# Smaller, spread loads of keys, values and queries, and later loads of the first expert's weights, in a kernel of attention and experts

## The chip, the cores and the metric

One core of a Trainium2 chip runs the kernel, with its five engines: TensorE (PE), VectorE (DVE), ScalarE (ACT), GpSimd (POOL) and SyncE (SP). SP computes nothing here and issues nearly all transfers. The metric is the device time of one execution in microseconds (us); the time of a kernel is the median of its runs.

## The reference, cut to what matters

```python
def attn(q, k, v):                       # (8, 8, 576, 64) each
    k_p = k.reshape(B, H, Sp, 8, D).mean(axis=3)      # keys pooled by 8
    v_p = v.reshape(B, H, Sp, 8, D).mean(axis=3)
    s = q @ k_p.T / sqrt(D)
    a = exp(s - max(s))
    return (a / sum(a)) @ v_p
x = attn(q, k, v)                        # 4608 tokens of 512
do = x @ w_skip > 0                      # only these tokens are computed
e = argmax(x[do] @ w_gate); gate = softmax(x[do] @ w_gate)[e]
y = gate * (relu(x[do] @ w1[e]) @ w2[e]) # 8 experts, 512 -> 1024 -> 512
out = x;  out[do] = x[do] + y
```

## The kernel before, in words

The 4608 tokens are 36 tiles of 128. The first part of the kernel (`attention`) runs a hand-made software pipeline with one turn per tile, t = 0 to 35. In turn t, TensorE makes the scores of tile t (L285), multiplies the exponentials of tile t - 2 with the pooled values (L325, L327) and transposes those of tile t - 1 (L309, L310). ScalarE copies the transposed exponentials out of PSUM (pT, L314) and takes the exponentials of tile t (e, L298); VectorE takes the minima before them (mn, L293) and normalises tile t - 3 (L341 to L346), whose 128x512 result SP stores to the output (L347). All engines run their instructions in the order in which the program was written, SP too: a transfer that waits holds up every transfer written behind it.

A batch b is 576 tokens, 4.5 tiles, and its first tile is FIRST[b] = 0, 4, 9, 13, 18, 22, 27, 31 (t0 below). For a batch there are loaded: the keys (L187, one transfer of 128 x 2304 floats, 1152 KB, into half of the tile `stage`), summed over 8 by four instructions of VectorE (kp, L194) in turns t0 - 5 to t0 - 2; the values (L206, 128 x 2048, 1024 KB, into the room of `hhi` or `hlo`, and two small ones, L208), summed by GpSimd (L216, L232) from turn t0 - 5 on. Queries come two tiles at a time (L270, 512 KB, into `qt`, `xhi` or `xlo`). A dictionary `loads` says in which turn a load is issued (`at(turn, f)`): keys at t0 - 8, values at t0 - 7, the queries of tiles 2i and 2i + 1 at 2i - 6, ahead of that turn's store.

The second part (`experts`) multiplies groups of tokens with an expert's weights. Those are split into a high and a low part, so each weight chunk (512 KB, eight chunks for an expert) is loaded to a slot of `stage` (L601 for the first expert), then copied by ScalarE (`high`, L607, two pieces of 128x512) and subtracted by GpSimd (`low`, L610, two pieces). The first expert's chunks come during the attention, in turns `wload(cc)` = 15, 17, 19, 21, 24, 26, 28, 30. Chunks 3, 4 and 5 use the slots of chunks 0, 1 and 2, so their loads wait until GpSimd has made the lows of those. The three planners `act`, `dve` and `gps` place such side work in turns by a ready turn, a last turn and a cost.

GpSimd also writes one row of a table for every token of a tile (L411, 33 such writes) as the routing of a group of tiles is done on VectorE; a small load of that table (L517, nids) waits for the first 18 tiles' writes, and GpSimd's L520 waits for it. After the attention GpSimd gathers from the table (L1064). From the ninth transfer on, each of SP's transfers waits on one of eight landing semaphores that are used in turn, so that at most eight transfers are under way.

Of the kernel before, what the change touches and what calls it, by code (L numbers as in the profile page):

```python
# [36 lines left out]
B, H, S, HD, POOL = 8, 8, 576, 64, 8  # L37
# [3 lines left out]
NT = NTOK // 128  # L41
# [7 lines left out]
LONG = max(SUMMED)  # L49
PICK, EARLY = 9, 18  # L50
PICKED = 15
LAST = 6
SCALE = 1.0 / (POOL * HD ** 0.5)
GMAX = max(GROUPS)
# [31 lines left out]
KL = SP - KM  # L86
# [17 lines left out]
def flat(ap):  # L104
    return ap.rearrange("p k n -> p (k n)")
# [51 lines left out]
def attention(tc, nc, q, k, vm, vr, cf, wg, w1, w2, whi, wlo, out, c, pay, offs, table, near, bufs, late, early, mb, fin, cfs):  # L157
    with ExitStack() as ctx:
# [19 lines left out]
        vls = [sp.tile([128, POOL, HD], F32, name=f"vl{i}") for i in range(2)]  # L178
        el = [sp.tile([128, 128], F32, name=f"el{i}") for i in range(2)]
        halves = [slice(hh * 64, hh * 64 + 64) for hh in range(2)]  # L180
        kts, kps, vts, vss, vTs, qts = {}, {}, {}, {}, {}, {}

        def load_k(b, gs=None):
            n = 4 * SP * POOL
            kts[b] = flat(stage)[:, b % 2 * n:b % 2 * n + n].rearrange("p (g k i) -> p g k i", g=4, i=POOL)
            if gs is None:
                nc.sync.dma_start(kts[b], k[b])  # L187
            for g in gs or ():
                nc.sync.dma_start(kts[b][:, g], k[b, :, g])

        def sum_k(b, g):
            if b not in kps:
                kps[b] = kp.tile([128, 4, SP], F32, name="kp")
            nc.vector.tensor_reduce(kps[b][:, g], kts[b][:, g], axis=AX.X, op=ALU.add)  # L194

        def keys(b, hh, gs=slice(0, 4)):

            r = halves[hh]
            nc.scalar.activation(kbd[b % 2][r, gs, hh * SP:(hh + 1) * SP], kps[b][r, gs], AF.Copy, scale=-SCALE)

        def load_v(b):
            vt = early("hhi" if b % 2 else "hlo", 128, POOL, 4 * HD)
            if b == 1:
                early("room1", 128, 8)
            vl = vls[b % 2]
            nc.sync.dma_start(vt, vm[b])  # L206
            for hh in range(2):
                nc.sync.dma_start(vl[hh * 64:hh * 64 + 4 * KL], vr[b, hh])  # L208
            vts[b] = vt, vl

        def sums(b):

            vt, vl = vts.pop(b)
            vss[b] = vs = vp.tile([128, 4 * HD], F32, name="vs")
            ls = wide[:, b % 2]
            add = lambda y, x, z: lambda: nc.gpsimd.tensor_tensor(y, x, z, ALU.add)  # L216
            first = [add(vt[:, i:i + 2], vt[:, i:i + 2], vt[:, i + 4:i + 6]) for i in (0, 2)]
            if b == 0:
                def half():
                    nc.vector.tensor_reduce(vs[:, 0:128], vt[:, :, 0:128].rearrange("p i n -> p n i"), axis=AX.X, op=ALU.add)  # L220

                def other(o):
                    for i in range(POOL):
                        nc.tensor.matmul(o, ident, vt[:, i, 128:256], start=(i == 0), stop=(i == POOL - 1))
                    nc.scalar.activation(vs[:, 128:256], o, AF.Copy)

                first = half, other
            else:
                first += [add(vt[:, 0:2], vt[:, 0:2], vt[:, 2:4]), add(vs, vt[:, 0], vt[:, 1])]
            small = [add(vl[:, 0:4], vl[:, 0:4], vl[:, 4:8]), add(vl[:, 0:2], vl[:, 0:2], vl[:, 2:4]),  # L230
                     add(ls, vl[:, 0], vl[:, 1]),
                     lambda: nc.gpsimd.tensor_tensor(vl4[b % 3][:, :, 0:HD], ls.unsqueeze(1).broadcast_to([128, 4, HD]),  # L232
                                                     left.unsqueeze(2).broadcast_to([128, 4, HD]), ALU.mult)]
            return first, small
# [12 lines left out]
        def values_in(b, gs=slice(0, 4), by=None):  # L247
            (by or nc.gpsimd.tensor_copy)(vb[b % 2][:, gs, 0:HD], vss[b].rearrange("p (g d) -> p g d", d=HD)[:, gs])
# [16 lines left out]
        def load_q(i, part=0):  # L265
            s = 128, QG, 4, 128
            if i not in qts:
                qts[i] = qp.tile(list(s), F32, name="qt") if i % 4 < 2 else early("xlo" if i % 4 > 2 else "xhi", *s)
            sl = (slice(None), slice(0, 1), slice(1, QG))[part]
            nc.sync.dma_start(qts[i][:, sl], q[i, :, sl])  # L270
# [46 lines left out]
        def values(t, pT, apart=False):  # L317
            if apart:
                os = [ps_s.tile([128, 512], F32, name="sc") for _ in range(2)]
            else:  # L320
                o = ps_o.tile([128, 2, 512], F32, name="o")
                os = [o[:, 0], o[:, 1]]
            for g in range(4):
                for hh, r, sl, b in blocks(t):
                    nc.tensor.matmul(os[hh][sl, g * VA:(g + 1) * VA], pT[r, g, sl], vb[b % 2][r, g, :], start=(g == 0), stop=False)  # L325
            for hh, r, sl, b in blocks(t):
                nc.tensor.matmul(os[hh][sl, 0:4 * VA], pT[r, 4, sl], vl4[b % 3][r].rearrange("p g c -> p (g c)"), start=False, stop=True)  # L327
            return [o_.unsqueeze(1) for o_ in os] if apart else [o]
# [268 lines left out]
        def room(cc):  # L597
            return 5 + cc % 3 if cc < 6 else cc - 6

        def load_first(cc):  # L600
            nc.sync.dma_start(chunk_view(stage[:, room(cc)], cc), chunk_src(w1, w2, expert(0), cc))  # L601

        def piece(w, cc, i):
            return w[0][:, cc, i * 512:i * 512 + 512] if cc < 4 else w[1][:, (cc - 4) * 2 + i, :]

        def high(cc, i):
            nc.scalar.activation(piece(whi, cc, i), stage[:, room(cc), i * 512:i * 512 + 512], AF.Copy)  # L607

        def low(cc, i, by=nc.gpsimd):
            return by.tensor_tensor(piece(wlo, cc, i), stage[:, room(cc), i * 512:i * 512 + 512],  # L610
                                    piece(whi, cc, i).bitcast(F32), ALU.subtract)
# [82 lines left out]
        act, dve, gps = Work(ACT), Work(DVE), Paced(GPS)  # L694

        def at(t, f):
            loads.setdefault(t, []).append(f)
# [3 lines left out]
        def later_low(cc, i):  # L701
            if cc * 2 + i > 12:
                rest.append(lambda v: low(cc, i, v))
            else:
                gps.add((now["t"] + 1, NT - 6, NT - 6, NT - 1, NT - 1)[max(cc - 2, 0)], wload(cc + 3) - 1 if cc < 3 else (NT - 3, NT - 1, NT + 9, NT + 9)[cc - 3],
                        1.25, lambda: low(cc, i))

        def adds(b, ready, last):
            first, small = sums(b)
            if b == 0:  # L710
                return first, small
            fs = [first[0], first[1], small[0], first[2], small[1], first[3], small[2], small[3]]
            for f, cost in zip(fs, (1.25, 1.25, 0.7, 1.25, 0.45, 0.7, 0.3, 0.7)):
                gps.add(ready, last, cost, f)

        def wload(cc):
            return PICKED + 9 * cc // 4 if cc < 8 else NT - 2

        for b in range(1, B):
            t0, slow = FIRST[b], int(b == 1)  # L720
            if b > 1:
                at(t0 - 8, lambda b=b: load_k(b))
                at(t0 - 7, lambda b=b: load_v(b))
            for g in range(4):
                dve.add([2, 2, 3, 3][g] if slow else t0 - 5 + g + (b == 2 and g < 2), [2, 2, 3, 3][g] if slow else t0 - 5 + g + (b == 2 and g < 2), 0.7,
                        lambda b=b, g=g: sum_k(b, g))
            for hh in range(2):
                act.add(t0 - 1 + slow / 2, t0 - 1, 0.45, lambda b=b, hh=hh: keys(b, hh))
            at(t0 - 6 + 5 * slow, lambda b=b, t0=t0, slow=slow: adds(b, t0 - 5 + 4 * slow, t0 - 3 + 3 * slow))
            turns[t0 + slow] = b  # L730
            gps.add(t0 - 2 + 3 * slow, t0 - 1 + 2 * slow, 0.6, lambda b=b: values_in(b))
        for i in range(2, NT // QG):
            at(max(2 * i - 6, i // 2 - 1), lambda i=i: load_q(i))
        at(PICKED, lambda: nc.sync.dma_start(cfs[:, 128:320], cf[:, -192:]))
        for cc in range(8):
            at(wload(cc), lambda cc=cc: load_first(cc))
            for i in range(2 if cc < LAST else 0):
                act.add(wload(cc) + (3 if cc < 3 else 4), min(wload(cc) + 6, NT - 2), 0.55, lambda cc=cc, i=i: (high(cc, i), later_low(cc, i)))

        nc.gpsimd.memset(init, NO_TOKEN)  # L740
        load_k(0, [0])
# [186 lines left out]
        os_[NT - 1] = values(NT - 1, pts.pop(NT - 1), True)  # L928
        for cc in range(LAST, 8):
            for i in range(2):  # L930
# [790 lines left out]
```

## Time and profile before

| what | value |
|---|---|
| time, median of 3 runs | 486.68 us (485.38 to 490.21) |
| time of the profiled execution | 490.18 us |
| its span, first to last instruction | 488.4 us |
| TensorE busy | 461.8 us (95%) |
| VectorE, ScalarE, GpSimd busy | 286.2, 234.3, 203.2 us |
| SP's transfers | 25728 packets, 71.73 MB, 40.8% of 16 DMA engines' span |

The span lies 1.8 us inside the time of the same execution. The attention fills the first 140 us or so, and the experts the rest. Every other time below is read from this one execution.

### The profile page before, as it was taken

The numbers are of one execution on the slowest core, as the hardware profiler recorded it, in microseconds if no ns is written. First come the engines' busy times: TensorE is split into PE (matmuls) and PEld (weight loads), VectorE is DVE, ScalarE is ACT, GpSimd is POOL, SyncE is SP. The second block draws the span as 40 slices with busy tenths as digits, with TensorE's granted clock in tenths as the row PEclk, the third lists the DMA queues.
The fourth block names the chain that finished last, engine by engine and source line by source line (L and its number), as shares of the span: only waits on it lengthen the run. The fifth ranks groups of instructions, "written<-read, shape, count | busy, mean of one in ns | idle before, by whom it ended". The sixth has DMA issues, their size and how long they took to land. (4 is left out here: it accounts for less than half of the span.)

```text
span 488.4 us, 12498 instructions
## 1 busy us (share of the span) xinstructions
PE 461.8 (95%) x4232; PEld 400.2 (82%) x4233; DVE 286.2 (59%) x690; ACT 234.3 (48%) x614; POOL 203.2 (42%) x267
## 2 busy tenths in 40 slices
PE   8999899998998898999999999999999999999993
PEld 7777677766678687898989989899998989889872
DVE  3678988888768445267666746323236452635563
ACT  4788798998772024154544624112215321424350
POOL 4588469988884331242303024331323322033020
PEclk9999999999999998999999999999999999999998
DMA  8999899967420174657571646111114551234110
GB/s 290 399 399 398 314 374 403 381 219 240 142 68 25 51 269 130 234 162 255 171 274 65 224 167 217 50 43 43 40 44 138 204 173 58 90 137 138 70 42 10
DMA packets 33214, 87.29 MB, mean 179 GB/s; under 512 B 6751, under 2 KB 7263, under 8 KB 31249
## 3 DMA queue, kind: packets, MB, share of 16 engines
q1 hardware_dynamic: 25728, 71.73, 40.8%
q0 software_dynamic: 7440, 14.99, 9.4%
q8 instruction: 24, 0.39, 0.3%
q14 instruction: 22, 0.17, 0.1%
HBM read 72.58 MB, written 20.19 MB: 190 GB/s over the span
## 5 line engine op out<-in xcount | busy, mean ns | idle before, releaser
L1376 PE MATMUL psl<-xhi,w1hi 128*128 128x256 f32 (+3 forms) x352 | 103.5, 294 | 0.3 <-PEq L1155 0.3
L1377 PE MATMUL psl<-xlo,w1hi 128*128 128x256 f32 (+3 forms) x352 | 103.4, 294 | 0.0
L1378 PE MATMUL psl<-xhi,w1lo 128*128 128x256 f32 (+3 forms) x352 | 103.4, 294 | 0.0
L1282 POOL DMA_INDIRECT out<-ring,slot x34 | 35.3, 1039 | 162.0 <-POOLq L1155 146.9
L1502 ACT ACTIVATE hhi<-psl 128x256 fp32r<-128x256 f32 (+3 forms) x88 | 36.2, 411 | 110.6 <-ACTq L1155 105.7
L1575 DVE SCALAR_TENSOR_TENSOR hlo<-psl,hhi 128x256 fp32r<-128x256 f32 (+1 forms) x88 | 38.1, 434 | 59.1 <-DVEq L1155 56.1
L298 ACT ACTIVATE e<-sc,mn 128x72 f32<-128x72 f32 x288 | 64.9, 343 | 12.0 <-DVE mn L293 11.7
L1376 PEld LDWEIGHTS psl<-xhi,w1hi 128*128 128x128 f32 x352 | 66.1, 188 | 1.1 <-issue 0.7
L1377 PEld LDWEIGHTS psl<-xlo,w1hi 128*128 128x128 f32 x352 | 66.1, 188 | 0.4
L1378 PEld LDWEIGHTS psl<-xhi,w1lo 128*128 128x128 f32 x352 | 66.1, 188 | 0.0
L1492 ACT ACTIVATE xhi<-psd 128x512 fp32r<-128x512 f32 x36 | 19.1, 599 | 77.5 <-ACTq L1155 77.5
L1277 POOL DMA_INDIRECT ring<-out,slot x36 | 40.3, 1119 | 21.2 <-issue 16.5
L1398 PE MATMUL psf<-w2hi,hhi 128*128 128x512 f32 x96 | 38.8, 404 | 2.3 <-PEq L1155 2.3
L1552 DVE TENSOR_TENSOR w2lo<-stage,w2hi 128x1024 fp32r<-128x1024 f32 x28 | 34.2, 1225 | 9.4 <-DVEq L1155 8.9
L411 POOL DMA_INDIRECT table<-pay,r_di x33 | 32.9, 996 | 15.0 <-DVE p_two L436 8.1
L1399 PE MATMUL psf<-w2lo,hhi 128*128 128x512 f32 x96 | 38.2, 398 | 0.0
L1400 PE MATMUL psf<-w2hi,hlo 128*128 128x512 f32 x96 | 37.9, 395 | 0.0
L293 DVE TENSOR_REDUCE mn<-sc 128x4 f32<-128x288 f32 x72 | 30.5, 452 | 10.4 <-PE sc L285 5.7
L1552 DVE TENSOR_TENSOR w1lo<-stage,w1hi 128x1024 fp32r<-128x1024 f32 x28 | 32.4, 1220 | 3.4 <-DVEq L1155 3.3
L1399 PE MATMUL mb<-w2lo,hhi 128*128 128x512 f32 x88 | 34.3, 390 | 0.0
L1398 PE MATMUL mb<-w2hi,hhi 128*128 128x512 f32 x88 | 34.3, 390 | 0.0
L1400 PE MATMUL mb<-w2hi,hlo 128*128 128x512 f32 x88 | 34.3, 390 | 0.0
(299 smaller groups left out, 943.3 us busy)
## 6 DMA issues: line engine op xcount, KB each, us to landing
stage<-in_w SPq DMA_DIRECT2D x64, 512.0 KB
out<-x SPq DMA_DIRECT2D x36, 256.0 KB
stage<-in_k SPq DMA_DIRECT2D x7, 1152.0 KB
qt<-in_q SPq DMA_DIRECT2D x9, 512.0 KB
hlo<-in_vm SPq DMA_DIRECT2D x4, 1024.0 KB
hhi<-in_vm SPq DMA_DIRECT2D x4, 1024.0 KB
xhi<-in_q SPq DMA_DIRECT2D x4, 512.0 KB
xlo<-in_q SPq DMA_DIRECT2D x4, 512.0 KB
```

Of the source, the lines that this page charges most:

```text
L298: nc.scalar.activation(e[:, g, hh * SP:(hh + 1) * SP], sc[:, h * SP:(h + 1) * SP], AF.Exp, bias=mn[:, 4 * i + h:4 * i + h + 1], scale=-1.0)
L1277: g.indirect_dma_start(ring[:, s % 6, 0:D], None, out, bass.IndirectOffsetOnAxis(ap=slot[:, s:s + 1], axis=0), bounds_check=NTOK - 1, oob_ ...
L1282: g.indirect_dma_start(out, bass.IndirectOffsetOnAxis(ap=offsets, axis=0), ring[:, s % 6, 0:D], None, bounds_check=NTOK - 1, oob_is_err=Fa ...
L1376: t.matmul(ps, whi[0][:, k, w], xhi[:, k, xs], start=(k == 0), stop=False)
L1377: t.matmul(ps, whi[0][:, k, w], xlo[:, k, xs], start=False, stop=False)
L1378: last = t.matmul(ps, wlo[0][:, k, w], xhi[:, k, xs], start=False, stop=(k == 3))
L1398: t.matmul(ps, hhi[:, k, sl], whi[1][:, k, :], start=(k == 0), stop=False)
L1399: t.matmul(ps, hhi[:, k, sl], wlo[1][:, k, :], start=False, stop=False)
L1400: last = t.matmul(ps, hlo[:, k, sl], whi[1][:, k, :], start=False, stop=(k == 7))
L1502: a.activation(hhi[:, f, xs], psL[f % 3][:, xs], AF.Relu).then_inc(sem["act"], 1)
L1552: v.tensor_tensor(chunk_of(wlo, c), chunk_view(stage[c], c), chunk_of(whi, c).bitcast(F32), ALU.subtract).then_inc(sem["wlo"], 1)
L1575: return v.scalar_tensor_tensor(out[:, f, :], psL[f % 3][:, xs], 0.0, hhi[:, f, xs].bitcast(F32), ALU.max, ALU.subtract)
```

## The change

Keys of batches 2 to 7 come in four loads of a quarter each (288 KB), one a turn from turn t0 - 8 on (for batch 2 the third and fourth a turn earlier). Their values come in two loads of half (512 KB: rows 0, 1, 4, 5 of the eight, then the others) and the two small ones, in turns t0 - 8, t0 - 7 and t0 - 6. Queries from tile 8 on come one tile at a time (256 KB), in turns 2i - 6 and 2i - 5. The first expert's chunks are issued in turns 19, 21, 23, 25, 27, 29, 30, 31, that is 4, 4, 4, 4, 3, 3, 2 and 1 turns later, and the last turn allowed for ScalarE's high pieces is nearer to the load. Bytes and arithmetic are the same; SP issues 38 transfers more.

```diff
 PICKED = 15
+CHUNKS = 19, 21, 23, 25, 27, 29, 30, 31
...
+        def load_k_part(b, g):
+            if g == 0:
+                load_k(b, [0])
+            else:
+                nc.sync.dma_start(kts[b][:, g], k[b, :, g])
...
+        def load_v_part(b, part):
+
+            if part == 0:
+                vts[b] = early("hhi" if b % 2 else "hlo", 128, POOL, 4 * HD), vls[b % 2]
+            vt, vl = vts[b]
+            if part < 2:
+                two = lambda y: y.rearrange("p (a i) n -> p a i n", a=2)[:, :, part * 2:part * 2 + 2]
+                nc.sync.dma_start(two(vt), two(vm[b]))
+            else:
+                for hh in range(2):
+                    nc.sync.dma_start(vl[hh * 64:hh * 64 + 4 * KL], vr[b, hh])
...
         def wload(cc):
-            return PICKED + 9 * cc // 4 if cc < 8 else NT - 2
+            return CHUNKS[cc] if cc < 8 else NT - 2
...
-                at(t0 - 8, lambda b=b: load_k(b))
-                at(t0 - 7, lambda b=b: load_v(b))
+                for g in range(4):
+                    at(t0 - 8 + g - (b == 2 and g > 1), lambda b=b, g=g: load_k_part(b, g))
+                for i in range(3):
+                    at(t0 - 8 + i, lambda b=b, i=i: load_v_part(b, i))
...
-            at(max(2 * i - 6, i // 2 - 1), lambda i=i: load_q(i))
+            if i < 4:
+                at(i // 2 - 1, lambda i=i: load_q(i))
+            else:
+                for part in range(2):
+                    at(2 * i - 6 + part, lambda i=i, part=part: load_q(i, part + 1))
...
-                act.add(wload(cc) + (3 if cc < 3 else 4), min(wload(cc) + 6, NT - 2), 0.55, lambda cc=cc, i=i: (high(cc, i), later_low(cc, i)))
+                act.add(wload(cc) + (3 if cc < 3 else 4), min(wload(cc) + (4 if cc < 3 else 5), NT - 2), 0.55, lambda cc=cc, i=i: (high(cc, i), later_low(cc, i)))
```

The order on TensorE and on VectorE does not change. On SP, the loads for batch 3 (turns 5 to 8) stood like this before, where in_k are keys, in_vm and in_vr values, and in_q queries:

```order
L187 DMA stage<-in_k 128x2304
L347 DMA out<-x 128x512
L206 DMA hhi<-in_vm 128x2048
L208 DMA vl_129<-in_vr 32x512 x2
L270 DMA xhi<-in_q 128x1024
```

and stand like this now:

```order
L190 DMA stage<-in_k 128x576
L225 DMA hhi<-in_vm 128x2x512
L289 DMA qt<-in_q 128x512
L366 DMA out<-x 128x512
L196 DMA stage<-in_k 128x576
L225 DMA hhi<-in_vm 128x2x512
L289 DMA xhi<-in_q 128x512
L366 DMA out<-x 128x512
L196 DMA stage<-in_k 128x576
L228 DMA vl_129<-in_vr 32x512 x2
```

Each turn now has a quarter of the keys, half of the values and one tile of queries between two stores, where one turn had all the keys and the next all the values.

On POOL, from batch 5's last sum to the first sums of batch 6 (w1lo are low pieces of the first expert, table the table writes), before:

```order
L232 TENSOR_TENSOR vl_125<-ls,cfs 128x4x64
L411 DMA table<-pay,r_di 36864x8
L610 TENSOR_TENSOR w1lo<-stage,w1hi 128x512 x2
L411 DMA table<-pay,r_di 36864x8
L248 COPY vb_122<-vs 128x4x64
L610 TENSOR_TENSOR w1lo<-stage,w1hi 128x512
L411 DMA table<-pay,r_di 36864x8
L216 TENSOR_TENSOR hlo<-hlo 128x512
L411 DMA table<-pay,r_di 36864x8
L610 TENSOR_TENSOR w1lo<-stage,w1hi 128x512
```

and now:

```order
L251 TENSOR_TENSOR vl_125<-ls,cfs 128x4x64
L430 DMA table<-pay,r_di 36864x8
L267 COPY vb_122<-vs 128x4x64
L430 DMA table<-pay,r_di 36864x8 x2
L235 TENSOR_TENSOR hlo<-hlo 128x512
L430 DMA table<-pay,r_di 36864x8
L235 TENSOR_TENSOR hlo<-hlo 128x512
```

Four low pieces leave this place; two of them come after batch 6's sums, and in all six stand ahead of L520 (now L539) in both programs.

On ACT, in turn 30 and the start of turn 31 (w1hi and w2hi are high pieces), before:

```order
L298 ACTIVATE e<-sc,mn 128x72 x8
L199 ACTIVATE kbd_120<-kp 64x4x72
L314 ACTIVATE pT<-pt 128x640
L303 ACTIVATE el_130<-e 128x2x32
L245 ACTIVATE vT<-pt 128x384
L607 ACTIVATE w2hi<-stage 128x512
```

and now:

```order
L317 ACTIVATE e<-sc,mn 128x72 x8
L206 ACTIVATE kbd_120<-kp 64x4x72
L626 ACTIVATE w1hi<-stage 128x512
L333 ACTIVATE pT<-pt 128x640
L322 ACTIVATE el_130<-e 128x2x32
L264 ACTIVATE vT<-pt 128x384
L626 ACTIVATE w2hi<-stage 128x512
```

One high piece more stands ahead of pT and vT there; three high pieces leave turns 18, 19 and 20, and turns 27, 33 and 34 get one more each, while turn 28 loses one.

## Rows read from the trace of the kernel before

**Rows 1.** Stretches: us, PE, PEld, DVE, ACT, POOL busy (x), clock, DMA share, GB/s.
```profile
0.00:10.00 10.00, 8.27 (x89) 7.67 (x91) 3.46 (x6) 4.01 (x13) 5.90 (x27) 1.00 0.84 282
10.00:60.00 50.00, 45.45 (x778) 35.49 (x778) 39.49 (x114) 39.59 (x150) 31.40 (x42) 1.00 0.99 377
60.00:100.00 40.00, 38.38 (x691) 30.09 (x691) 35.22 (x102) 36.88 (x137) 34.28 (x41) 1.00 0.99 377
100.00:150.00 50.00, 44.43 (x723) 34.07 (x722) 39.27 (x150) 38.62 (x128) 42.41 (x50) 1.00 0.47 156
```

**Rows 2.** Waits, 0 to 155 us: us in total, times, longest.
```profile
PEld pt L309 <- issue: 14.5, 32, 0.5
...
POOL hhi L216 <- DMA hhi<-in_vm: 8.2, 2, 5.5
...
DVE kp L194 <- DMA stage<-in_k: 5.5, 3, 3.6
```

**Rows 3.** Timeline of PE, scores of two turns: start, us, line, [idle before].
```profile
44.90 1.15 PE L285 MATMUL sc<-kbd,qt 128*128 128x144 f32 x8
...
47.76 1.15 PE L285 MATMUL sc<-kbd,qt 128*128 128x144 f32 x8
```

**Rows 4.** Timeline, turns 19 and 20: a high piece, a transpose and its copy.
```profile
77.67 0.62 ACT L607 ACTIVATE w1hi<-stage 128x512 fp32r<-128x512 f32 x1
...
79.47 0.27 PE L310 MATMUL pt<-cfs,el 128*128 128x128 f32 x1
...
79.81 0.76 ACT L314 ACTIVATE pT<-pt 128x640 f32<-128x640 f32 x1
```

**Rows 5.** Timeline, turn 30: VectorE, GpSimd and TensorE.
```profile
114.07 1.27 POOL L216 TENSOR_TENSOR hhi<-hhi 128x512 f32<-128x512 f32 x1
114.11 1.27 DVE L465 TENSOR_TENSOR mb<-offs,cfs 128x8 f32<-128x8 f32 x1
...
116.26 0.75 PE L325 MATMUL o<-vb,pT 64*64 64x74 f32 x32 [1.39 <-DVE mb L467]
```

**Rows 6.** Timeline, turn 31: what waits for vT, and a gap.
```profile
120.72 0.41 PE L255 MATMUL mb<-wgs,vT 128*64 128x18 f32 x8 [0.18 <-ACT vT L245]
...
122.67 0.31 PE L325 MATMUL o<-vb,pT 64*64 64x74 f32 x3 [0.45 <-issue]
```

**Rows 7.** Timeline, batch 3's keys: their issue and their first sum.
```profile
26.59 0.33 SPq L187 DMA_DIRECT2D stage<-in_k  x1
...
39.23 0.74 DVE L194 TENSOR_REDUCE kp<-stage 128x72 f32<-128x576 f32 x1
```

**Rows 8.** Timeline, SP and POOL in turns 27 to 31.
```profile
104.39 2.51 POOL L610 TENSOR_TENSOR w1lo<-stage,w1hi 128x512 fp32r<-128x512 f32 x2
...
106.92 0.41 SPq L601 DMA_DIRECT2D stage<-in_w  x1
...
112.36 0.99 POOL L411 DMA_INDIRECT table<-pay,r_di  x1 [0.17 <-issue]
...
116.95 0.39 SPq L517 DMA_DIRECT2D nids<-table  x1
...
118.99 0.29 POOL L520 TENSOR_SCALAR nslot<-nids,less 128x2 int32<-128x2 f32 x1 [1.26 <-DMA nids<-table]
```

**Rows 9.** Timeline of POOL, last table write and the gather.
```profile
149.08 0.97 POOL L411 DMA_INDIRECT table<-pay,r_di  x1 [0.30 <-issue]
...
156.34 1.07 POOL L1064 DMA_INDIRECT stage<-table,s_coli  x1 [6.29 <-DVE s_at L1075]
```

**Rows 10.** Timeline of ACT, exponentials of four turns.
```profile
32.69 1.80 ACT L298 ACTIVATE e<-sc,mn 128x72 f32<-128x72 f32 x8 [0.21 <-DVE mn L293]
...
35.78 1.80 ACT L298 ACTIVATE e<-sc,mn 128x72 f32<-128x72 f32 x8 [0.44 <-DVE mn L293]
...
61.94 1.80 ACT L298 ACTIVATE e<-sc,mn 128x72 f32<-128x72 f32 x8 [0.43 <-DVE mn L293]
64.57 1.80 ACT L298 ACTIVATE e<-sc,mn 128x72 f32<-128x72 f32 x8
```

## The prediction, made before the changed kernel was run

> **What bounds the kernel now.** The change touches the attention's 36 turns alone, so I read that stretch first. In the table of stretches the 16 DMA engines are fully taken from 10 to 100 us (share 0.99, 377 GB/s) and half idle from 100 to 150 us (0.47) [rows 1]. That is what the change works on, and it looks like the bound. But TensorE is busy 45.45 of 50 and 38.38 of 40 us in the same two stretches [rows 1]. So the second view is the list of waits: who of the computing engines waits for a load? Up to 155 us these waits are small. The largest are GpSimd's for values, 8.2 us in two waits with one of 5.5, and VectorE's for keys, 5.5 us in three [rows 2]. The three of VectorE are those for batch 0, and the 5.5 us of GpSimd is for batch 1; both are loaded ahead of the first turn, and the change leaves them as they are. TensorE and ScalarE show no wait for a load. TensorE's most frequent gap is 14.5 us in 32 turns ahead of the transposes, with nothing to wait for [rows 2].
>
> Third, the timeline of a turn. With the DMA engines full, the scores of one plain turn begin at 44.90 us and those of the next at 47.76: 2.86 us [rows 3]. In turns 19 and 20 the transposes end at 79.47 + 0.27 = 79.74 us, and ScalarE's copy starts at 79.81 [rows 4]. TensorE sets the pace, with ScalarE close behind; a load that comes earlier meets an engine that isn't waiting for it.
>
> **The loads in smaller pieces.** 38 more issues on SP cost about 0.4 us each (the issues in [rows 7, 8] took 0.33 to 0.41), 15 us of an engine that computes nothing. That costs nothing as long as each load lands before its use. The tightest user is VectorE's sum of keys: a quarter is now issued three turns ahead of its sum, some 8.6 us at 2.86 a turn. For batch 3, all keys were issued at 26.59 us and first summed at 39.23, 12.6 us later [rows 7]. Now the first quarter stands in the same turn, behind more transfers, of which at most eight are under way. Eight of some 290 KB are 2.3 MB, 6 us at 377 GB/s [rows 1], so it may be issued up to 39.23 - 6 = 33 us, over 6 us later than before. The later quarters are issued up to three turns later and summed up to three turns later. Gain 0, cost 0. If that cover went, VectorE would wait, then ScalarE and TensorE, one for one.
>
> Smaller rows may also move more slowly. The trace gives two rates for a full queue: 377 / 0.99 = 381 GB/s where large loads ran, and 282 / 0.84 = 336 in the first 10 us, which hold quarters of keys, single tiles of queries and the start-up [rows 1]. The later stretch had stores of 256 KB and small values among its loads at all times, so I take the value near 381; 336 is the other end. A rule speaks against the change here. The Trainium skill (DMA: Bandwidth & Descriptors, Bandwidth) says to batch transfers to at least 1 MiB for at least 75% of the peak; the keys go from 1152 to 288 KB. By the rule the queue would fall behind, which is the first rival below; by the row, with several transfers under way at once, it keeps its rate.
>
> **The chunks, 1 to 4 turns later.** What is late next? Loads of chunks 3 to 5 wait for GpSimd's lows: chunk 5 was issued at 106.92 us, right after two lows that began at 104.39 and took 2.51 [rows 8]. GpSimd has six lows to make ahead of L520 in both programs, but three leave the stretch after 80 us, where it may now run dry until the second routing group's rows are ready. That delays L520 by 0 to 2.5 us: three lows of 1.26 are 3.8, less the 1.26 it idled there waiting for nids [rows 8]. I take 1, between the ends, since nids itself should come earlier (its last table write moves ahead of lows). At the tail GpSimd has room: its last table write ends at 150.05 us, the gather starts at 156.34 after 6.29 us of idling, and a write lands within 3.6 us or so (112.36 + 0.99 to 116.95, where nids is let go) [rows 8, 9]. That leaves 156.34 - 150.05 - 3.6 = 2.7 us, more than the 2.5. Cost 0. The last chunks' loads come at about 120 us, into a half-empty queue [rows 1], and are used eight us later or more.
>
> **ScalarE's high pieces**, 0.62 us each [rows 4]. Three leave turns 18 to 20, but there ScalarE waits for TensorE's transposes anyway (79.74 against 79.81) [rows 4]: gain 0 to 0.3, I take 0.1. The one added in turn 27 stands ahead of a copy that nobody waits for. Those in 33 and 34 fill gaps of about half a us ahead of the exponentials. The one in turn 30 pushes vT, and TensorE's L255 waited for vT already (0.18 us) [rows 6]; but 2 us later TensorE stops for 0.45 us with nothing to wait for, which may swallow it [rows 6]. Cost 0 to 0.62, I take 0.2.
>
> **One collision that moves.** At 114.11 us VectorE's L465, an operation on 8 columns, takes 1.27 us. GpSimd's sum began at 114.07 and also took 1.27: the one ended with the other [rows 5]. TensorE then waits 1.39 us for VectorE, and this is on the path [rows 5]. The Trainium skill (SBUF — State Buffer, SBUF: two separate sides) calls it an exclusive lock between the two engines, held for the whole instruction, where VectorE has two operands in SBUF; the trace agrees with 1.27 against 1.27. GpSimd's order ahead of this changes, so L465 will meet another place of another operation: it waits for 0 to 1.27 us, and the gain is 0 to 1.1. GpSimd should still be among its sums there, so I take a gain of 0.4, below the middle.
>
> **Sum**, against the profiled execution of 490.18 us (1.8 us of it outside the span): - 0.1 + 0.2 - 0.4 = - 0.3, so 489.9. That execution is the slowest of the three runs; scaled to their median, 486.68 x 489.9 / 490.18 = 486.4 us. One per cent, 4.9 us, is about what a measurement of this kernel can tell from no change.
>
> **Rivals.** First, the small loads slow the queue: slower. Place: keys of batches 3 and 4, at 26 to 60 us. The 50 us from 10 to 60 moved 377 x 50 = 18.9 MB; at 336 GB/s that takes 56 us, 6 us more [rows 1]. It decides from the point where the extra lag passes the 6 us or so that the keys have to spare; as the queue stays full to 100 us, the lag would grow to 11 us there, so some 5 us reach TensorE: 491.7. For it: the queue is full for 90 us, and the rate of the first stretch. Against it: that stretch also holds the first microsecond, when nothing had been issued, and its share was not full. The 1 MiB rule of the Trainium skill (DMA: Bandwidth & Descriptors, Bandwidth) is on its side.
>
> Second, the full queue costs turns in a way that the waits don't name: faster. In the rows of ScalarE, a plain turn under a full queue took 35.78 - 32.69 = 3.09 us, a later one 64.57 - 61.94 = 2.63 [rows 10]. If half of that difference, 0.23 us, belonged to the queue in each of some 24 turns before 100 us, the change could give back up to 5.5: 481.2. Against it: TensorE's own distance under the same load is 2.86 [rows 3], and VectorE had two key sums between those exponentials.
>
> Third, GpSimd's lows come so late that chunk 5 is not there when ScalarE takes it in turn 33: SP, ScalarE and then TensorE wait. ScalarE should come to it near 128 us, and the load takes some 3, so the lows of chunk 2 would have to end after 125 us. I expect them about 119, and 122 with the 2.5 us above; at 127 it would cost 2 us: 488.7, within one per cent.
>
> **Chances.** My forecast 0.80, first rival 0.07, second 0.08, third 0.05. The first two end beyond one per cent, the third within: faster 0.08, no difference 0.85, slower 0.07. The likeliest case spans the unknown terms: - 1.4 (0.3 and 1.1 gained) to + 0.6, and the runs of before spread 4.8 us around their median; a median of three moves perhaps 1.5. That is 483.8 to 488.8; towards the slow side I go to 489.6 for the third rival and a part of the first.
>
> **What would show it.** Right: scores 2.86 us apart in plain turns, no wait of TensorE or ScalarE for a load, DMA share below 0.99 before 75 us and higher after 100, L465 of another length, the gather waiting for VectorE as before. Wrong: VectorE's sums of keys waiting for loads (first rival), plain turns well under 2.86 (second), ScalarE's high pieces waiting for `stage` (third), or GpSimd's last table write landing after VectorE is ready.

## The result, and the profile after

| kernel | median, runs | before in the same group of runs | ratio, 95% interval |
|---|---|---|---|
| the changed kernel | 490.31 us (488.78 to 493.62), 13 | 486.75 us (485.38 to 490.21), 13 | 1.0063 [1.0043, 1.0082] |
| the changed kernel, measured a second time | 484.81 us (483.49 to 487.41), 12 | 483.74 us (482.65 to 489.70), 23 | 1.0009 [0.9981, 1.0037] |

The ratio is an estimate from the single runs, not the quotient of the medians, which is 1.0073 and 1.0022. 486.4 us was forecast, in a range to 489.6. The first measurement lies 0.7 us above that range: 0.63 per cent slower, less than the one per cent set as the bound, but beyond its interval. The second measurement, made as the last experiment, shows no difference that its interval can tell from none. Both are of the same program, and their intervals don't overlap; most of what follows is about why.

The profiled execution of the first measurement took 492.04 us (span 490.2), that of the second 483.49 us (span 481.7). All of the difference lies in the attention. The first product of the experts, on TensorE, starts at 179.39 us in the one, at 170.46 us in the other, and at 174.51 us in the trace of the kernel before (timeline of TensorE: first trace, second, kernel before):

```profile
179.39 0.39 PE L1401 MATMUL psl<-xhi,w1hi 128*128 128x320 f32 x1 [0.31 <-PEq L1180]
```

```profile
170.46 0.38 PE L1401 MATMUL psl<-xhi,w1hi 128*128 128x320 f32 x1 [0.31 <-PEq L1180]
```

```profile
174.51 0.39 PE L1376 MATMUL psl<-xhi,w1hi 128*128 128x320 f32 x1 [0.31 <-PEq L1155]
```

From there to the end it is 490.2 - 179.4 = 310.8 us, 481.7 - 170.5 = 311.2 and 488.4 - 174.5 = 313.9. So against the trace of before, the first trace of the change lost 4.9 us in the attention and the second gained 4. The spans of before and of the first trace lie only 1.8 us apart because the trace of before lost some 3 us among the experts, where its clock fell (shown below); every other trace of this document needs 310.8 to 311.6 us from that product to the end.

The table of stretches, as in [rows 1]: start and end in us, length, busy time and instructions of PE, PEld, DVE, ACT and POOL, granted clock, DMA share, GB/s. First the first trace of the changed kernel:

```profile
0.00:10.00 10.00, 8.27 (x89) 7.63 (x90) 3.46 (x6) 3.98 (x13) 5.92 (x27) 1.00 0.81 281
10.00:60.00 50.00, 44.65 (x733) 34.70 (x732) 38.36 (x111) 38.05 (x142) 30.02 (x41) 1.00 0.99 350
60.00:100.00 40.00, 38.84 (x687) 30.34 (x685) 33.93 (x99) 34.41 (x127) 30.59 (x38) 0.96 0.98 331
100.00:150.00 50.00, 44.50 (x738) 32.97 (x736) 39.10 (x141) 42.20 (x142) 44.33 (x52) 0.97 0.62 212
```

and the second:

```profile
10.00:60.00 50.00, 45.14 (x773) 35.19 (x773) 40.14 (x117) 39.57 (x148) 31.74 (x42) 1.00 1.00 355
60.00:100.00 40.00, 38.65 (x694) 30.14 (x692) 35.70 (x100) 36.52 (x134) 31.21 (x37) 1.00 0.99 343
100.00:150.00 50.00, 46.45 (x768) 38.18 (x768) 43.74 (x176) 39.73 (x131) 44.13 (x51) 1.00 0.59 207
```

Both traces agree on what the change does to the transfers: the DMA engines are as full as before between 10 and 100 us, but move 350 and 331 GB/s (355 and 343) where they moved 377 [rows 1], and from 100 to 150 us more is left to move. They disagree on TensorE: 733 instructions against 773 from 10 to 60 us, and a granted clock of 0.96 and 0.97 in stretches in which the second trace has 1.00.

The waits up to 155 us, as in [rows 2], of the first trace:

```profile
PEld pt L328 <- issue: 15.0, 33, 0.9
ACT pT L333 <- PE pt L329: 10.7, 10, 2.9
POOL vl L235 <- DMA vl<-in_vr: 8.5, 3, 4.9
DVE kp L201 <- DMA stage<-in_k: 5.1, 2, 3.5
PEld o L346 <- issue: 3.5, 5, 1.1
PEld o L344 <- issue: 3.5, 7, 1.2
PE o L346 <- issue: 1.6, 4, 0.6
```

and of the second:

```profile
PEld pt L328 <- issue: 14.4, 32, 0.5
POOL vl L235 <- DMA vl<-in_vr: 9.5, 5, 4.1
DVE kp L201 <- DMA stage<-in_k: 6.0, 4, 3.4
ACT pT L333 <- PE pt L329: 2.7, 5, 0.8
```

In neither do TensorE or ScalarE wait for a load. What the first trace has, and the second lacks among its longest waits, are stops of TensorE inside the products with the values (L344, L346) with nothing to wait for, 3.5 us in 7 and 3.5 in 5 ahead of weight loads, and behind them ScalarE, which waits for the transposes 10.7 us instead of 2.7. (The longest of L344, 1.2 us, is not a stop: at 119.19 us the row of the product itself waits 1.01 us for VectorE.) The kernel before has such stops too, if fewer; there the 1.6 us is again a wait for VectorE [rows 5]:

```profile
PEld o L325 <- issue: 3.0, 6, 1.6
PEld o L327 <- issue: 1.9, 5, 0.6
```

### The profile page after: what moved, and what is told of

Same layout as the page of the kernel before. It is cut to its first block, busy times and chain, and to the rows that moved or that the text cites. A ratio compares the mean times of both kernels' runs of the same rounds, so it can differ in the third digit from the quotient of the medians.

```text
span 490.2 us, 12541 instructions
## 1 busy us (share of the span) xinstructions
PE 464.6 (95%) x4232; PEld 401.8 (82%) x4233; DVE 286.4 (58%) x690; ACT 234.8 (48%) x614; POOL 206.1 (42%) x267
## 5 line engine op out<-in xcount | busy, mean ns | idle before, releaser
L1307 POOL DMA_INDIRECT out<-ring,slot x34 | 36.4, 1069 | 156.4 <-POOLq L1180 145.8
```

Source lines behind the costliest of these rows:

```text
L1307: g.indirect_dma_start(out, bass.IndirectOffsetOnAxis(ap=offsets, axis=0), ring[:, s % 6, 0:D], None, bounds_check=NTOK - 1, oob_is_err=Fa ...
```

## Where the first trace loses its time

Measured from minima to minima, mainly three places of the attention are longer in the first trace than in the trace of before: turn 9 by 1.2 us, turns 13 and 14 by 1.7, turn 31 by 2.3. In the second trace turns 9, 13 and 14 are as long as before, and turn 31 is 1.3 us shorter.

**A stop in turn 9.** The timeline of TensorE, first trace: 16 of the 32 products of a turn, then nothing for 0.86 us, then the rest.

```profile
43.33 0.58 PE L344 MATMUL o<-vb,pT 64*64 64x74 f32 x16
44.78 0.42 PE L344 MATMUL o<-vb,pT 64*64 64x74 f32 x11 [0.86 <-issue]
```

The second trace, same place:

```profile
42.36 0.65 PE L344 MATMUL o<-vb,pT 64*64 64x74 f32 x28
42.84 0.41 PE L346 MATMUL o<-vl,pT 64*64 64x296 f32 x1
```

The stop goes with the queue that the page calls "instruction". In 2.5 us windows of the DMA view (queue, kind: packets, MB, share), first the kernel before from 38.5 to 41 us, then the first trace of the changed kernel from 41 to 43.5:

```profile
q8 instruction: 1, 0.02, 2.6%
```

```profile
q8 instruction: 1, 0.02, 2.5%
```

In the first trace of the changed kernel there is no such packet from 38.5 to 41. The packet has 16384 bytes, and up to 145 us one comes every 3.4 to 13.6 us. I took its start from the packets of all traces but one (in whole_rows below, turn 9 lies elsewhere), in us from the start of turn 9's minima, beside the length of that turn (minima to minima):

| traces | packet | turn 9 |
|---|---|---|
| ten: before, the second of the change, and eight experiments | -2.4 to -1.4 | 3.50 in every one |
| last_late | -0.6 | 4.00 |
| light_after, light_before | -0.5 | 4.17, 4.25 |
| first_late | -0.3 | 4.27 |
| spaced, sp_free, the first of the change | -0.1 | 4.53, 4.54, 4.71 |
| chunks_again | 0.0 | 4.81 |
| mid_late | +0.4 | 5.07 |

A packet that comes 1 us later makes the turn 1 us longer, once it is late enough, and it stops at the same place: the row that resumes counts 11 or 12 of the 32 products in each of the five traces whose rows I compared. In all nine late traces TensorE resumes 2.3 to 2.5 us after the start of the packet. The same nine, and none of the ten others, stop once more in turn 11, and resume there 2.4 to 2.7 us after the start of the next packet. I read this as TensorE running out of instructions. The Trainium skill (Runtime: NRT & Kernel Launch, Instruction fetch mechanics) describes such refills in blocks of 16 KiB over a DMA queue and calls their cost mostly hidden; the size agrees with the packets here, and the cost does not in these nine traces: 0.5 to 1.6 us in one turn.

Turn 9 stands ahead of anything that the chunks' turns change: in chunks_again, spaced, sp_free and mid_late, all is written up to there as in the kernel before, and light_before, a kernel of before with lighter chunks, stops too. So this stop can come in either kernel. Why the packet is late is open. GpSimd's clearing of the table, 1.2 MB over another queue, begins 0.2 to 2.9 us ahead of turn 9 in all of these traces: the packet starts 0.5 to 2.9 us after its first packet where it is late, and 0.6 to 2.2 us before it elsewhere. But in seven of the nine late traces the clearing begins less than 1.4 us ahead of the turn, after the place at which the packet comes elsewhere, so it is at most a part of the reason; no run moved it.

**Half the clock, twice.** The stretches 60 to 65 and 125 to 130 us of the first trace:

```profile
60.00:65.00 5.00, 5.00 (x76) 4.24 (x77) 3.41 (x11) 3.28 (x14) 4.96 (x7) 0.66 1.02 352
125.00:130.00 5.00, 4.48 (x33) 2.96 (x25) 1.33 (x5) 2.15 (x9) 4.38 (x5) 0.66 0.94 284
```

The clock went to its lower level, 1.2 instead of 2.4 GHz, for part of each; the second trace has 1.00 in both. Ahead of the first, TensorE had waited 1.48 us for VectorE's routing; in the second trace it waited 1.42 us there and kept its clock, so the wait alone doesn't decide. The kernel before had lost its clock in another place:

```profile
190.00:195.00 5.00, 3.87 (x10) 3.08 (x11) 4.16 (x5) 3.63 (x4) 0.00 (x0) 0.66 0.34 117
```

In the first trace of the change, turns 13 and 14 take 1.7 us longer than in the second trace. But the lower clock does not explain the time of the first measurement: its four executions with the highest mean clock, 0.997, took 489.64 to 490.96 us, around the median of all. (At that mean no stretch is lost but the end: the traces of spaced and chunks_again have 0.997, and full clock up to their last 3 us.)

**Turn 31.** First trace; the second row of it has eight products in 2.06 us, which take 0.71 in the second trace:

```profile
124.53 0.77 PE L344 MATMUL o<-vb,pT 64*64 64x74 f32 x30
125.72 2.06 PE L346 MATMUL o<-vl,pT 64*64 64x296 f32 x8 [0.43 <-issue]
127.71 1.11 PE L328 MATMUL pt<-cfs,e 128*128 128x128 f32 x4
...
129.07 0.70 ACT L333 ACTIVATE pT<-pt 128x640 f32<-128x640 f32 x1 [2.85 <-PE pt L329]
```

```profile
120.23 0.75 PE L344 MATMUL o<-vb,pT 64*64 64x74 f32 x32
120.77 0.71 PE L346 MATMUL o<-vl,pT 64*64 64x296 f32 x8
121.41 0.66 PE L328 MATMUL pt<-cfs,e 128*128 128x128 f32 x4
```

Stops, then the lower clock (0.66 above): the turn is 3.6 us longer than in the second trace. The first of these stops ends 2.5 us after the start of a packet (125.72 - 123.22), as in turn 9. The kernel before has stops in the turns from 31 on as well, but the one in [rows 6] ends at 122.67 us, and the packets next to it start at 112.74 and 122.80: late packets don't account for all of them.

## The experiments

Kernels of one group ran on one chip beside their own runs of the kernel before. "Chunks later" means the line CHUNKS of the change with its narrower window for ScalarE. Two theories came out of the first trace: the loads in smaller pieces (A), or the chunks that come later (B).

**First group (before: 487.20 us).** loads_only is the changed kernel with these two lines as before:

```diff
-            return CHUNKS[cc] if cc < 8 else NT - 2
+            return PICKED + 9 * cc // 4 if cc < 8 else NT - 2
...
-min(wload(cc) + (4 if cc < 3 else 5), NT - 2)
+min(wload(cc) + 6, NT - 2)
```

> The loads split and spread as in the change, but the first expert's chunks and ScalarE's high pieces where they were before. Theory A (the small rows fill the queue for longer, and TensorE stops in the full queue): ratio to before 1.004 to 1.007, rate under a full share 340 to 355 GB/s between 10 and 100 us, and a stop of TensorE of 0.8 us or more with nothing to wait for near turn 9. Theory B (the later chunks and the high piece in turn 30 cost it): ratio 0.998 to 1.002. Theory C (both parts, about half each): 1.002 to 1.004.

Measured: 487.01 us, 1.0010 [0.9981, 1.0038].

chunks_only is the kernel before with the opposite edit of the same lines.

> The kernel before, with the chunks and ScalarE's high pieces in the turns of the change and the loads in one piece. Theory A: ratio 0.998 to 1.002, and turns 30 to 32 as far apart as before. Theory B: 1.004 to 1.007, with TensorE losing some 2 us between 123 and 130 us. Theory C: 1.002 to 1.004.

Measured: 490.92 us (486.83 to 493.50), 1.0078 [1.0050, 1.0106]. Within this group the cost belongs to the later chunks with their narrower window, and not to the smaller loads, although those took the full queue to 360 / 1.01 = 356 GB/s in loads_only. Its profiled execution, 486.95 us, was among its fastest, and shows no loss of that size.

whole_rows keeps the number of pieces but cuts by partitions, so that rows stay whole:

```diff
-                nc.sync.dma_start(kts[b][:, g], k[b, :, g])
+            nc.sync.dma_start(kts[b][32 * g:32 * g + 32], k[b, 32 * g:32 * g + 32])
...
+                nc.sync.dma_start(vt[64 * part:64 * part + 64], vm[b, 64 * part:64 * part + 64])
```

> The loads split in as many pieces as in the change and spread over the turns, but by partitions (keys 4 x 32, two a turn; values and queries 2 x 64), so that the rows are as long as before; chunks as before. If the short rows cost the time (A by rows): ratio 0.998 to 1.002 and 375 to 385 GB/s under a full share. If the number of transfers or their places cost it (A by count): 1.004 to 1.007.

Measured: 515.81 us, 1.0592 [1.0546, 1.0638], far outside both. The table of stretches shows why:

```profile
10.00:60.00 50.00, 41.39 (x641) 32.49 (x639) 30.82 (x74) 32.57 (x124) 27.00 (x38) 0.93 1.03 299
60.00:100.00 40.00, 31.15 (x483) 23.82 (x481) 25.90 (x85) 25.59 (x94) 19.62 (x24) 0.87 1.03 264
```

The queue is full and moves only 299 and 264 GB/s. Loads of 32 or 64 partitions cost far more than short rows do; the question for which it was made stays unanswered.

small_old issues all pieces in the turn of the old load:

```diff
-                    at(t0 - 8 + g - (b == 2 and g > 1), lambda b=b, g=g: load_k_part(b, g))
+                    at(t0 - 8, lambda b=b, g=g: load_k_part(b, g))
```

> The same small loads with the same short rows, but all pieces of a load issued in the turn in which the whole load was issued before; chunks as before. A by rows: ratio 1.004 to 1.007, 340 to 355 GB/s under a full share. If the spreading over the turns costs it: 0.998 to 1.002. Theory B: 0.998 to 1.002 as well, together with loads_only.

Measured: 488.49 us, 1.0026 [1.0000, 1.0052]: 0.3 per cent, at the edge of none, when all pieces come at once, and 0.1 when they are spread (loads_only); the two intervals overlap, so they can't be told apart.

**Second group (before: 485.03 us): which chunks?**

chunks_wide is chunks_only without its narrower window:

```diff
-min(wload(cc) + (4 if cc < 3 else 5), NT - 2)
+min(wload(cc) + 6, NT - 2)
```

> The kernel before with the chunks loaded in the later turns, but the last turn allowed for ScalarE's high pieces as before, so that they stand one a turn (30, 31, 32, 33, 34) instead of two in turn 30. Theory P (the second high piece in turn 30, which pushes vT and TensorE): ratio to before 0.998 to 1.002. Theory L (GpSimd's lows of chunks 0 to 2, now beside its routing work in turns 16 to 22): 1.005 to 1.010. Theory E (the loads of chunks 5 to 7 at the attention's end): 1.005 to 1.010.

Measured: 489.00 us, 1.0094 [1.0058, 1.0130].

first_late, against chunks_only:

```diff
-CHUNKS = 19, 21, 23, 25, 27, 29, 30, 31
+CHUNKS = 19, 21, 23, 25, 26, 27, 28, 30
```

> The kernel before with chunks 0 to 4 in turns 19, 21, 23, 25, 26 and chunks 5 to 7 in turns 27, 28, 30 (1, 0 and 0 later), high pieces with the narrow window: two in turn 30 and two in turn 31. Theory P: 1.005 to 1.010. Theory L: 1.005 to 1.010. Theory E: 0.998 to 1.002.

Measured: 493.18 us, 1.0180 [1.0132, 1.0228]. In both, some chunk's load is written ahead of the last pieces of the chunk that had its slot, so these are taken from another chunk, and wait for its load (timelines of POOL and ACT in first_late, then of POOL in chunks_wide):

```profile
110.87 1.26 POOL L611 TENSOR_TENSOR w1lo<-stage,w1hi 128x512 fp32r<-128x512 f32 x1 [3.82 <-DMA stage<-in_w]
113.95 0.63 ACT L608 ACTIVATE w1hi<-stage 128x512 fp32r<-128x512 f32 x1 [7.87 <-DMA stage<-in_w]
```

```profile
123.67 1.27 POOL L611 TENSOR_TENSOR w1lo<-stage,w1hi 128x512 fp32r<-128x512 f32 x1 [4.21 <-DMA stage<-in_w]
```

So they don't tell the theories apart. They show two other things: what ScalarE's wait for a late chunk costs (TensorE in first_late then waits 6.46 us for the exponentials), and that the change's narrower window is needed with its turns.

```profile
115.48 1.33 PE L286 MATMUL sc<-kbd,xhi 128*128 128x144 f32 x4 [6.46 <-ACT e L299]
```

last_late, against chunks_only:

```diff
-CHUNKS = 19, 21, 23, 25, 27, 29, 30, 31
+CHUNKS = 15, 17, 19, 21, 24, 29, 30, 31
```

> The kernel before with only chunks 5 to 7 later (turns 29, 30, 31 instead of 26, 28, 30); no high piece in turns 30 and 31. Theory P: 0.998 to 1.002. Theory L: 0.998 to 1.002. Theory E: 1.005 to 1.010.

Measured: 484.70 us, 0.9993 [0.9967, 1.0019].

window_only, against the kernel before:

```diff
-min(wload(cc) + 6, NT - 2)
+min(wload(cc) + (4 if cc < 3 else 5), NT - 2)
```

> The kernel before with only the narrower window of ScalarE's high pieces, which moves one piece from turn 23 to 21 and one low a turn earlier. All three theories: 0.998 to 1.002.

Measured: 486.22 us, 1.0021 [0.9994, 1.0048]. last_late seemed to clear chunks 5 to 7. But none of the four traces of this group has a stop from turn 31 on, where the traces of the first group have them, so this group may have cleared them for another reason.

**Third group (before: 487.13 us): what about chunks 0 to 5?** All four are chunks_only with one line changed. spaced:

```diff
-                act.add(wload(cc) + (3 if cc < 3 else 4),
+                act.add(wload(cc) + (3 if cc < 4 else 4),
```

> The kernel of chunks_only with chunk 3's high pieces allowed one turn earlier, so that one of them moves out of turn 31, where two stood ahead of batch 7's vT. Theory V (the two high pieces in front of vT): ratio to before 0.998 to 1.003. Theory S (SP waits at chunk 5's load for GpSimd's lows of chunk 2, and the stores behind it come late): 1.005 to 1.010. Theory D (the loads and stores that come together at 120 to 130 us stop TensorE): 1.005 to 1.010.

sp_free:

```diff
-CHUNKS = 19, 21, 23, 25, 27, 29, 30, 31
+CHUNKS = 19, 21, 23, 25, 27, 30, 29, 31
```

> The kernel of chunks_only with chunk 6 in turn 29 and chunk 5 in turn 30, so that SP comes to chunk 5's load after the lows of chunk 2 are done, and no store waits behind it. Theory V: 1.005 to 1.010. Theory S: 0.998 to 1.003. Theory D: 1.005 to 1.010.

mid_late:

```diff
-CHUNKS = 19, 21, 23, 25, 27, 29, 30, 31
+CHUNKS = 15, 17, 19, 25, 27, 29, 30, 31
```

> Chunks 0 to 2 in the turns of before, chunks 3 to 7 in the turns of the change. Two high pieces in front of batch 7's vT, the lows of chunk 2 still late, chunk 5's load waits for them. Theories V, S and D: 1.005 to 1.010. If it is the lateness of chunks 0 to 2 by itself that costs (their lows and highs beside the routing work of turns 20 to 26): 0.998 to 1.003.

two_later:

```diff
-CHUNKS = 19, 21, 23, 25, 27, 29, 30, 31
+CHUNKS = 17, 19, 21, 23, 25, 27, 28, 30
```

> Chunks 0 to 5 two turns later or less (17, 19, 21, 23, 25, 27), chunks 6 and 7 as before. Two high pieces in front of batch 7's vT, but the lows of chunk 2 are done before SP comes to chunk 5's load, and the loads at 120 to 130 us are those of before. Theory V: 1.005 to 1.010. Theories S and D: 0.998 to 1.003.

Measured: spaced 489.91 us, 1.0052 [1.0020, 1.0085]; sp_free 489.58 us, 1.0035 [1.0008, 1.0063]; mid_late 489.31 us, 1.0051 [1.0020, 1.0082]; two_later 490.06 us, 1.0062 [1.0035, 1.0090]. spaced speaks against V, two_later against S and D, and mid_late against the lateness of chunks 0 to 2 by itself; sp_free lies between its two forecasts. All four are slower, and no single place of a chunk explains them.

**Fourth group (before: 489.77 us): traffic or order?** The same edit in the kernel before and in chunks_only:

```diff
-            nc.sync.dma_start(chunk_view(stage[:, room(cc)], cc), chunk_src(w1, w2, expert(0), cc))
+            n = 128 if cc < 4 else 64
+            nc.sync.dma_start(chunk_view(stage[:, room(cc)], cc)[..., :n], chunk_src(w1, w2, expert(0), cc)[..., :n])
...
+        nc.gpsimd.memset(stage[:, 5:8], 0.0)
```

> The kernel before, but each load of a chunk of the first expert brings only an eighth of its columns (64 KB instead of 512), so the first expert computes with other weights; three slots are cleared once at the start (some us of GpSimd). This is the partner of light_chunks. If the later chunks cost their time by traffic (theory D): light_chunks and light_before within 0.2 per cent of each other. If they cost it by the order of ScalarE's, GpSimd's and SP's work (theories V, S, L): light_chunks 0.4 per cent or more above light_before.

> The kernel of chunks_only with the same small chunk loads (an eighth of the columns, so the first expert computes with other weights) and the same clearing. Theory D: as light_before within 0.2 per cent. Theories V, S, L: 0.4 per cent or more above light_before.

Measured: light_before 488.85 us, 0.9977 [0.9951, 1.0003]; light_chunks 490.16 us, 0.9998 [0.9973, 1.0023]. They are 0.21 per cent apart, where 0.2 was to speak for traffic and 0.4 for order: undecided. highs_late, against the kernel before:

```diff
-                act.add(wload(cc) + (3 if cc < 3 else 4), min(wload(cc) + 6, NT - 2), 0.55, lambda cc=cc, i=i: (high(cc, i), later_low(cc, i)))
+                ready = (18, 20, 22, 29, 31, 33)[cc]
+                act.add(ready, ready + (1 if cc > 2 else 3), 0.55, lambda cc=cc, i=i: (high(cc, i), later_low(cc, i)))
```

> The kernel before, all loads and lows where they were, but the high pieces of chunks 3 to 5 as late as in mid_late (turns 29, two in 31, 32, 33, 34). If ScalarE's late pieces are the cause (V, in the wider form that any piece in turns 31 to 34 pushes TensorE): ratio to before 1.004 to 1.008. If the later loads or lows are: 0.998 to 1.002.

Measured: 489.05 us, 0.9979 [0.9952, 1.0006]. No cost of ScalarE's later pieces shows.

> The kernel of chunks_only once more, beside the three others on the same chip: 1.005 to 1.010 under every theory; a second trace, in which theory D expects TensorE to stop for over 1 us with nothing to wait for between 120 and 130 us, and theories V and S a wait on ScalarE or VectorE there.

Measured: 491.75 us, 1.0037 [1.0009, 1.0065], half of what the same kernel cost in the first group, and below what was expected under every theory. Its trace stops in turns 9, 11 and 31, among others.

**Fifth group (before: 483.74 us): the changed kernel itself**, and the same with the light chunks.

> The changed kernel, but each load of a chunk of the first expert brings an eighth of its columns (the first expert computes with other weights), and three slots are cleared once. Theory D (the traffic of the later chunks): ratio to before 0.996 to 1.001, at least 0.3 per cent below after_again. Theories of order (S, L): 1.003 to 1.008, within 0.2 per cent of after_again.

> The changed kernel once more, beside light_after on the same chip: 1.004 to 1.008 under both theories. Its second trace shows which of the three losses of the first trace (turn 9, the half clock at 62 us, the half clock at 126 us) return: those that belong to the change should, those of one execution need not.

Measured: light_after 484.89 us, 1.0026 [1.0003, 1.0049]; after_again 484.81 us, 1.0009 [0.9981, 1.0037]. Both miss. None of the three losses of the first trace returned in that of after_again, and with them went the cost; there was nothing left for lighter chunks to take away. The kernel before was faster here too: the third and the fifth group ran on the same chip, and it took 487.13 us in the one and 483.74 in the other.

**What is shown, and what stays open.** Shown: the time between the two traces of the changed kernel is lost to stops of TensorE and to the lower clock, in turns 9, 13, 14, 31 and some others, and the stop of turn 9 follows a late instruction packet, one for one. Shown too, in the first group: the smaller loads don't cost the time, the later chunks do. Not shown: that the 3.6 us between the medians of the first measurement are made of the same stops, as only one of its 13 executions was traced; and why the later chunks would bring more of them. As a measure I summed, from 10 to 160 us, the distances of over 0.25 us between the starts of two neighbouring instructions in the products with the values of which the later waits for no semaphore. In groups one, three and four and the first measurement, the eight traces with chunks 3 and 4 later hold 2.0, 2.1, 2.3, 4.4, 5.0, 5.2, 6.0 and 6.1 us (mean 4.1); the seven other traces outside the fifth group, less whole_rows and the two that mix chunks, hold 1.3, 1.3, 2.0, 2.2, 2.2, 2.6 and 5.0 (2.4); after_again holds 0 and light_after 1.6. That looks like a hint of 1.7 us, on one execution of each. But it counts the stops of turns 9 and 11, which stand ahead of anything that the chunks change: from turn 12 on the means are 2.4 and 1.7, a difference of 0.7 us that is well inside the spread of either set (1.1 to 3.3 and 0 to 2.6). A cause would need the instruction packets of many executions.

## Why the prediction was wrong, point by point

**What bounds the kernel**: right. TensorE sets the pace, the scores of plain turns are 2.85 us apart in both traces, and no load is waited for on TensorE or ScalarE in either. But [rows 2] also holds stops with nothing to wait for (14.5 us in 32 ahead of the transposes), and [rows 6] one of 0.45 us. I took them for a fixed habit and the latter even for slack that "may swallow" a later vT. Those ahead of the transposes are fixed: 14.4 to 15.0 us in 32 or 33 in all three traces, 0.45 us each. The one of [rows 6] is not: the second trace has none there, the first stops twice. **This is the step that failed: the sum had no term for stops of TensorE without a wait**, neither for their size nor for their changing from run to run, and none for a stretch at the lower clock. In their place the first trace shows 1.2 us in turn 9, 1.7 in turns 13 and 14 at half the clock, and 2.3 in turn 31, against the trace of before. How much of the 3.6 us between the medians they make is open; the lower clock is not needed for it (above).

**The loads in smaller pieces**: gain 0 and cost 0 held (loads_only 1.0010). The rate did not: I took a value near 381 GB/s, with 336 as the other end, and it is 350 / 0.99 = 354 and 331 / 0.98 = 338. So one sign of being right failed: the share of the DMA engines did not fall below 0.99 before 75 us (1.00 from 10 to 75 us in both traces). After 100 us it rose as forecast, 0.62 and 0.59 against 0.47. The 1 MiB rule of the Trainium skill (DMA: Bandwidth & Descriptors, Bandwidth) was on the right side here by its sign. The lag it makes still stays within the reserve: VectorE's waits for keys are 5.1 and 6.0 us against 5.5 in [rows 2]. So the first rival was nearer with its rate (354 GB/s in its own place, 338 after it, against its 336), and wrong in its consequence.

**The chunks later**: cost 0 was wrong in the first group, where the later chunks alone gave 1.0078, and the cost isn't where I looked for it. The term rested on lows, landings and the tail, and those came out as follows. GpSimd's L520 (now L539) begins at 123.13 us against 118.99 [rows 8], while turn 31's minima move from 120.74 to 123.73 us, so it is 123.13 - 118.99 - 2.99 = 1.2 us later in its turn (1 was taken); in the second trace it is 2.4 later (the upper end was 2.5). The tail hides it as forecast; the gather still waits for VectorE, 7.2 us in the first trace and 2.1 in the second. SP issues chunk 5's load at 122.84 us, as soon as its lows end (120.29 + 2.52 = 122.81), and ScalarE takes it at 133.14 without waiting: the third rival didn't come.

**ScalarE's high pieces**: vT is later by 0.58 - 0.18 = 0.40 us [rows 6] in both traces, where 0.2 was taken and 0.62 was the end.

```profile
124.05 0.41 PE L274 MATMUL mb<-wgs,vT 128*64 128x18 f32 x8 [0.58 <-ACT vT L264]
```

```profile
119.70 0.41 PE L274 MATMUL mb<-wgs,vT 128*64 128x18 f32 x8 [0.58 <-ACT vT L264]
```

**The collision**: L465 (now L484) takes 0.908 us in the first trace and 0.659 in the second against 1.27 [rows 5], a gain of 0.36 and 0.61 where 0.4 was taken.

**The range and the chances**: no difference by more than one per cent had 0.85, and both measurements lie there. The range gave 1.5 us to the measurement. The same program was 0.63 per cent slower than before in one group and 0.09 in another, 2.6 us of 487 apart. Against the second measurement the forecast of no change, and its 0.06 per cent, holds; against the first its upper end is 0.7 us short. That the second measurement hits is in part luck: there the losses stayed away for which the sum had no term.

## What to carry to other kernels

A stop "issue" on the engine that sets the pace is a cost like a wait, and not slack. If it stands inside a run of equal instructions, look for the 16 KB packets of the instruction queue some 2.5 us ahead of where it ends, and compare two executions before a change is blamed or praised. Where an effect of half a per cent is to be judged, measure both kernels in more than one group of runs: here two groups gave 1.0063 and 1.0009 for the same program, each with an interval of 0.3 per cent or less to either side. Cut loads by columns rather than by partitions: pieces of the columns cost the kernel 0.1 per cent, which can't be told from none, as many pieces of the partitions 5.9.

## What was not expected of the hardware

- TensorE stops when the 16 KB instruction packet comes late: turn 9 takes 3.50 us where the packet starts 1.4 us or more ahead of its minima, and 4.00 to 5.07 us where it starts 0.6 us ahead to 0.4 behind. This is inferred from 19 traces that agree, not from a record of TensorE's own.
- Loads over 32 and 64 partitions move 299 and 264 GB/s in a full queue, those of the same bytes and the same number over 128 partitions 360 and 333 (loads_only, same stretches). The Trainium skill (DMA: Bandwidth & Descriptors, Rules for kernel authors) advises against two transfers to halves of the partitions; the runs agree, by 29 us of the kernel.
- Smaller loads with rows of 2048 and 2304 bytes instead of 4096 to 9216 go with a full queue that is 7 and 11 per cent slower (354 and 338 against 381 GB/s); loads_only has 360 / 1.01 = 356 and 333 / 0.99 = 336. The second number is not the rows' alone: between 60 and 100 us chunks_only, with the long rows, moved 350 / 0.98 = 357.

```profile
60.00:100.00 40.00, 37.68 (x688) 29.35 (x687) 34.75 (x100) 35.26 (x130) 30.80 (x37) 1.00 0.98 350
```
